# Induced attention and channel mix on one core: the running maximum meets across partitions on VectorE instead of TensorE

## The chip, the core and the metric

The kernel runs on one core of a Trainium2 chip. The metric is the device time of one execution in microseconds (us). Before the change three runs took 1166.9, 1169.22 and 1169.98 us, so the median is 1169.22. Engines go by the names of the profile: PE is TensorE (PEld its weight loads), DVE is VectorE, ACT is ScalarE, POOL is GpSimd, SP is SyncE, which issues the transfers.

## The reference

`x` holds 4 sequences of 12608 tokens with 128 channels, `inducing` 32 vectors. First the 32 vectors attend to all tokens of a sequence, which gives h (32 x 128); then each token attends to h. A channel mix follows on that result.

```python
def mab(q, kv):
    s = scale * (q @ kv.transpose(0, 2, 1))
    s = s - s.max(-1, keepdims=True)
    a = np.exp(s)
    a /= a.sum(-1, keepdims=True) + 1e-09
    return a @ kv
h = mab(I, x)                  # 32 queries over 12608 tokens
x = mab(x, h)                  # every token over 32 vectors
x_prev = x shifted by one token (zero in front)
xk = mu_k * x + (1.0 - mu_k) * x_prev
xr = mu_r * x + (1.0 - mu_r) * x_prev
k = np.maximum(xk @ w_k, 0.0)  # 1024 wide
v = k * k @ w_v
out = v / (1.0 + np.exp(-(xr @ w_r)))
```

The change concerns the maximum `s.max` of the first attention, the one over all tokens of a sequence, for each of the 32 vectors.

## The kernel before

A sequence is cut into 6 full blocks of 2048 tokens (block 0 to 5) and a remainder of 320. A block has four groups of 512 tokens, so a sequence has 25 groups. The channel mix handles a group in four units, each for 256 of the 1024 hidden channels; 4 sequences make 400 units, and the program is one long loop over units with the order of all engines written out by hand.

In unit n the loop emits, in this order: for a group that is done, the gate `L809` on VectorE (product of the finished bank of `ps_v` and the sigmoid); `up`, four TensorE products `L773`, `L775` into one of two pairs of banks of `ps_a`; the entries of a table `early` (filled by `soon`); `square`: VectorE takes the positive part (`L785`, ps_a to k_t), ScalarE squares twice (`L790` rounded, `L791` exact; in some units `L787` on VectorE in place of `L790`), GpSimd subtracts the two (`L793`, both inputs in SBUF); in one of four units `zgate`, the gate's product `L762`, `L763` into a bank of `ps_v`, of which there are two; `store` (`L820` and transfers); `down` of the unit four earlier, six products `L804` into the same `ps_v`; and then the entries of a table `events` (filled by `at`). An engine works through its instructions in this order, and SP its transfers.

The tables hold the attention work of later blocks. `stage_b` is the second attention of the block that the channel mix needs soon; its `low` (`L654`) splits off the low part of the weights from a bank `pb_b`, and its `spread` has SP send them to the tiles R that `up` reads. `stage_a` is the first attention of the next sequence, one block each 12 units, so it runs 18 times: blocks 0 to 5 of sequences 1 to 3 (sequence 0 has a head of its own, in which GpSimd has no subtractions). One such run is called a pass here. A pass starts at t; its scores are written in unit t + 9 to 128 partitions, 32 for each of the four groups of tokens, and `L364` takes the maximum over the free axis, which leaves one number per partition. The four numbers of one inducing vector lie in partitions m, m + 32, m + 64 and m + 96 and have to meet, since all four groups are to share one maximum. In block 5 the remainder's maximum `mxt` joins first (`L370`).

They meet in `common` and `running`. `common` has TensorE multiply the column of maxima, read as 128 equal columns, by the identity (`L371`; the profile counts two matmuls for it), so that each partition holds all 128 numbers in bank `pb_b`. `running` adds the constant `apart` (zero where the vector is the same, a huge negative number elsewhere, `L377`), and reduces by maximum (`L380`) together with the running maximum of earlier blocks, which lies in column 128 of the same tile; `L382` scales it to the bias `nb` of the exponentials in unit t + 15. `common` stands in `early` of unit t + 11, between `up` and `down`; in block 5 of unit t + 12; `running` in `events` of the same unit.

Of the kernel before, what the change touches and what calls it, by code (L numbers as in the profile page):

```python
# [8 lines left out]
F32 = mybir.dt.float32  # L9
# [4 lines left out]
ALU = mybir.AluOpType  # L14
AX = mybir.AxisListType
# [4 lines left out]
def kernel(  # L20
# [11 lines left out]
    nc = tc.nc  # L32
    B, N, C = x.shape
    M = inducing.shape[0]
    F = w_k.shape[1]
    P = 128
# [11 lines left out]
    scale = 1.0 / float(C) ** 0.5  # L48

    const = ctx.enter_context(tc.tile_pool(name="const", bufs=1))  # L50
# [4 lines left out]
    sm = ctx.enter_context(tc.tile_pool(name="sm", bufs=2))  # L55
# [7 lines left out]
    def pb_tile(bank=None):  # L63

        return pb.tile([P, G], F32, name="pb_" + (bank or next(banks)))


    ident = const.tile([P, P], F32, name="ident")
# [70 lines left out]
    omur = const.tile([P, 1], F32, name="omur")  # L139
    stack = const.tile([P, Q, M], F32, name="stack")  # L140
    stack_f = stack.rearrange("p i m -> p (i m)")
    apart = const.tile([P, P], F32, name="apart")

    def constants():
        for dst, src in ((omuk, muk), (omur, mur)):
            nc.vector.tensor_scalar(out=dst, in0=src, scalar1=-1.0, scalar2=1.0,
                                    op0=ALU.mult, op1=ALU.add)
        nc.vector.tensor_reduce(out=stack[:, 0, :], in_=ident.rearrange("p (i m) -> p m i", i=Q),
                                op=ALU.add, axis=AX.X)
        for i in range(1, Q):  # L150
            nc.vector.tensor_copy(out=stack[:, i, :], in_=stack[:, 0, :])
        nc.vector.tensor_scalar(out=apart, in0=stack_f, scalar1=-1.0, scalar2=3.0e38, op0=ALU.add, op1=ALU.mult)

    wvh = const.tile([P, FC, C], F32R, name="wvh")
    wvl = const.tile([P, FC, C], F32R, name="wvl")
# [158 lines left out]
    def stage_a(b, j, at, t):  # L314
# [2 lines left out]

        S = batches[b]
        L = {}
        tail = j == NBLK - 2
# [41 lines left out]
            L["mx"] = mx  # L365

        def common():
            ps = pb_tile("b")
            if tail:
                nc.vector.tensor_tensor(out=L["mx"], in0=L["mx"], in1=L["mxt"], op=ALU.max)  # L370
            nc.tensor.matmul(out=ps[:, :P], lhsT=L["mx"].broadcast_to([P, P]), rhs=ident,  # L371
                             start=True, stop=True)
            L["cp"] = ps

        def running():
            mk = S.mk if j > 0 else sm.tile([P, P + 1], F32, name="mkr", bufs=2)
            nc.vector.tensor_tensor(out=mk[:, :P], in0=L["cp"][:, :P], in1=apart, op=ALU.add)  # L377
            S.mk = sm.tile([P, P + 1], F32, name="mkr", bufs=2)
            L["mx"] = S.mk[:, P:P + 1]
            nc.vector.tensor_reduce(out=L["mx"], in_=mk[:, :P + (j > 0)], op=ALU.max, axis=AX.X)  # L380
            L["nb"] = sm.tile([P, 1], F32, name="nb")
            nc.vector.tensor_scalar(out=L["nb"], in0=L["mx"], scalar1=-scale, scalar2=None, op0=ALU.mult)  # L382

        def expo():
            e1t = st.tile([P, G], F32, name="e1t", bufs=1)
# [61 lines left out]
        if tail:  # L447
            at(t + 5, t_tr)
            soon(t + 11, t_scores)
        at(t + 9, scores)  # L450
        soon(t + 11 + tail, common)
        at(t + 11 + tail, running)
        at(t + 15, expo)
        at(t + 17, etrans)
# [440 lines left out]
    def head():  # L895
# [6 lines left out]
        for k in range(NBLK):  # L902
            ab[k].maxi()
            ab[k].expo()
            place(PARTS[k][0])
            if k > 0:
                ab[k - 1].hmm()
            if k == last:
                maxes()
            if k > 0:  # L910
                ab[k - 1].acc()
            if k == 0:
                constants()
            if k + 2 < NBLK:
                ab[k + 2].tr()
            place(PARTS[k][1])
            ab[k].etrans()
            ab[k].ecopy()
            ab[k].sums()
            if k < last:  # L920
                ab[k + 1].scores()
            place(PARTS[k][2])
# [13 lines left out]
    def at(n, f):  # L936
        events.setdefault(n, []).append(f)

    def soon(n, f):
        early.setdefault(n, []).append(f)  # L940
# [41 lines left out]
    for b in range(B):  # L982
        t = b * UB + (4 if b == 0 else 0)
        for j in range(NBLK - 1):
            s = t + SEG * j
            high_vector |= {s + 4, s + 8}
            if b + 1 < B:
                stage_a(b + 1, j, at, s)
            stage_b(b, j + 1, at, s + 1)
        if b + 1 < B:  # L990
            s = t + SEG * (NBLK - 1)
            combine(b + 1, at, s)
            stage_b(b + 1, 0, at, s + 13)
# [73 lines left out]
```

## Time and profile before

| | |
|---|---|
| median of 3 runs | 1169.22 us |
| profiled execution | 1165.47 us, its span 1163.7 us |
| mean granted TensorE clock | 0.996 |
| PE busy | 1114.2 us (96%) |
| ACT busy | 970.9 us (83%) |
| POOL busy | 947.7 us (81%) |
| DVE busy | 934.3 us (80%) |

The profile is of one execution. In its rows a group of instructions stands with line, engine, operation, tiles (written <- read), shape and count, then busy time and the mean of one in ns, then the idle time of the engine before them with what ended it. A row of the timeline begins with start and length in us. A row of a line's view gives shortest, median and longest duration in ns. The end of a matmul is modelled, so neighbours on PE overlap in the rows.

### The profile page before, as it was taken

The page shows a single profiled execution, that of the slowest core. Times are in us where ns is not written, and L with a number is a line of the kernel's source. Part 1 is how long each engine was busy: PE and PEld are TensorE (multiplying, and loading weights), DVE is VectorE, ACT ScalarE, POOL GpSimd, SP SyncE. Part 2 cuts the span into 40 slices and gives each one's busy share as a digit, 9 for nine tenths or more (in the row PEclk, how much of TensorE's full clock was granted, in tenths as well). Part 3 has the DMA queues.
Part 4 walks back from the last instruction along what each step waited for, and adds up shares of the span by engine and source line. Part 5 has one row for each costly group of instructions (what it writes and reads, how often), then busy time and mean ns, then how long its engine had stood idle before and what let it go on. Part 6 is the DMA issues. An engine that isn't in the chain of part 4 may idle for free.

```text
span 1163.7 us, 17576 instructions
## 1 busy us (share of the span) xinstructions
PE 1114.2 (96%) x5746; PEld 834.2 (72%) x5746; DVE 934.3 (80%) x1259; ACT 970.9 (83%) x1107; POOL 947.7 (81%) x413
## 2 busy tenths in 40 slices
PE   7779999999999999999999999999999999999997
PEld 5456777776677777777767777777768777777886
DVE  5778889887878888888787889897787888887665
ACT  5478888887888888788978988888789888889996
POOL 1158888888787888888879888888878899999997
PEclk9989999999999999999999999999999999999999
DMA  9112554544226455465043554645304314432231
GB/s 288 50 32 75 128 118 106 109 117 92 39 58 134 108 105 123 108 135 120 5 76 74 118 125 104 134 96 124 45 15 82 63 34 73 73 64 46 43 46 34
DMA packets 273515, 102.31 MB, mean 88 GB/s; under 512 B 232816, under 2 KB 248336, under 8 KB 271120
## 3 DMA queue, kind: packets, MB, share of 16 engines
q1 hardware_dynamic: 273088, 101.17, 40.5%
q8 instruction: 46, 0.75, 0.3%
q14 instruction: 45, 0.37, 0.1%
q10 hardware_dynamic: 336, 0.02, 0.0%
HBM read 28.07 MB, written 25.82 MB: 46 GB/s over the span
## 4 chain that ended last, share of the span: by engine, by line
PE 61%; DVE 15%; ACT 8%; SPq 6%; issue 5%; DMA 4%; DVEq 0%; ACTq 0%
PE ps_v L804 31%; PE ps_a L773 11%; PE ps_a L775 10%; DVE k_t L785 5%; SPq L336 2%; DMA out_dram<-ot 2%; ACT kh L790 2%; SPq L827 2%; PE pb_a L426 1%; PE pb_b L610 1%; PE ps_v L762 1%; PE ps_v L763 1%; SPq L664 1%; ACT k_t L791 1%; PE pb_a L361 1%
## 5 line engine op out<-in xcount | busy, mean ns | idle before, releaser
L793 POOL TENSOR_TENSOR kl<-k_t,kh 128x1024 fp32r<-128x1024 f32 (+2 forms) x400 | 939.0, 2375 | 169.0 <-ACT k_t L791 148.9
L785 DVE TENSOR_SCALAR k_t<-ps_a 128x1024 f32<-128x1024 f32 (+1 forms) x400 | 480.9, 1202 | 155.5 <-PE ps_a L775 144.1
L791 ACT ACTIVATE k_t<-k_t 128x1024 f32<-128x1024 f32 (+1 forms) x400 | 418.2, 1048 | 45.5 <-DVE kh L787 34.3
L790 ACT ACTIVATE kh<-k_t 128x1024 fp32r<-128x1024 f32 (+1 forms) x352 | 365.9, 1040 | 104.5 <-DVE k_t L785 57.8
L773 PE MATMUL ps_a<-R,W 128*128 128x512 f32 (+1 forms) x800 | 325.9, 408 | 4.7 <-DMA R<-al 3.4
L775 PE MATMUL ps_a<-R,W 128*128 128x512 f32 (+1 forms) x800 | 313.6, 392 | 0.0
L804 PE MATMUL ps_v<-kh,wvh 128*128 128x512 f32 (+1 forms) x800 | 251.9, 396 | 5.5 <-ACT rT L765 5.0
L804 PE MATMUL ps_v<-kl,wvh 128*128 128x512 f32 (+1 forms) x800 | 249.2, 393 | 0.0
L804 PE MATMUL ps_v<-kh,wvl 128*128 128x512 f32 (+1 forms) x800 | 249.0, 392 | 0.0
L773 PEld LDWEIGHTS ps_a<-R,W 128*128 128x128 f32 x800 | 151.2, 189 | 82.3 <-issue 22.4
L804 PEld LDWEIGHTS ps_v<-kh,wvh 128*128 128x128 f32 x800 | 147.9, 189 | 42.3 <-ACT rT L765 10.1
L804 PEld LDWEIGHTS ps_v<-kl,wvh 128*128 128x128 f32 x800 | 149.6, 188 | 35.5 <-POOL kl L793 0.3
L804 PEld LDWEIGHTS ps_v<-kh,wvl 128*128 128x128 f32 x800 | 149.8, 188 | 34.9
L775 PEld LDWEIGHTS ps_a<-R,W 128*128 128x128 f32 x800 | 151.1, 189 | 29.8
L820 DVE STREAM_TRANSPOSE ot<-oT 128x512 f32<-128x512 f32 x96 | 67.4, 702 | 12.2 <-DMA out_dram<-ot 11.3
L809 DVE TENSOR_TENSOR oT<-ps_v,rT 128x512 f32<-128x512 f32 (+1 forms) x100 | 66.7, 667 | 2.4 <-PE ps_v L804 0.2
L787 DVE SCALAR_TENSOR_TENSOR kh<-ps_a,k_t 128x1024 fp32r<-128x1024 f32 x48 | 58.8, 1225 | 5.4 <-PE ps_v L804 0.5
L765 ACT ACTIVATE rT<-ps_v 128x512 f32<-128x512 f32 (+1 forms) x99 | 57.2, 578 | 0.3
L333 DVE STREAM_TRANSPOSE xs<-xb 128x512 f32<-128x512 f32 x72 | 50.0, 695 | 0.3
L765 ACT ACT_TABLE_LOAD x31 | 39.8, 1283 | 0.6
L762 PE MATMUL ps_v<-R,W 128*128 128x512 f32 (+1 forms) x99 | 38.9, 393 | 0.0
L763 PE MATMUL ps_v<-R,W 128*128 128x512 f32 (+1 forms) x99 | 38.7, 391 | 0.0
(194 smaller groups left out, 643.6 us busy)
## 6 DMA issues: line engine op xcount, KB each, us to landing
out_dram<-ot SPq DMA_DIRECT2D x92, 256.0 KB, 4.4
xb<-in_x_dram SPq DMA_DIRECT2D x18, 1024.0 KB, 5.3
xt<-xs SPq DMA_DIRECT2D x288, 64.0 KB, 2.0
R<-ah SPq DMA_DIRECT2D x184, 64.0 KB, 2.0
R<-al SPq DMA_DIRECT2D x184, 64.0 KB, 2.0
kh<-in_x_dram SPq DMA_DIRECT2D x4, 512.0 KB, 8.2
kl<-in_x_dram SPq DMA_DIRECT2D x4, 512.0 KB, 6.4
xb<-in_x_dram SPq DMA_DIRECT2D x8, 256.0 KB, 5.4
```

What stands on the lines that cost most here:

```text
L762: nc.tensor.matmul(out=ps[:, :w], lhsT=S.W[0][:, F:WF], rhs=R[:, 1:w + 1], start=True, stop=False)
L765: nc.scalar.activation(out=self.rT, in_=ps[:, :w], func=AF.Sigmoid)
L773: nc.tensor.matmul(out=ps[:, c, :w], lhsT=S.W[0][:, cs], rhs=R[:, 1:w + 1], start=True, stop=False)
L775: nc.tensor.matmul(out=ps[:, c, :w], lhsT=S.W[1][:, cs], rhs=R[:, 0:w], start=False, stop=True)
L785: nc.vector.tensor_scalar(out=k, in0=self.ps[:, :, :w], scalar1=0.0, scalar2=None, op0=ALU.max)
L787: nc.vector.scalar_tensor_tensor(out=kh, in0=self.ps[:, :, :w], scalar=0.0, in1=k, op0=ALU.max, op1=ALU.mult)
L790: nc.scalar.activation(out=kh, in_=k, func=AF.Square)
L791: nc.scalar.activation(out=k, in_=k, func=AF.Square)
L793: return lambda eng, a, z: eng.tensor_tensor(out=kl[:, :, a:z], in0=k[:, :, a:z], in1=kh.bitcast(F32)[:, :, a:z], op=ALU.subtract)
L804: nc.tensor.matmul(out=self.v, lhsT=wt[:, fc, :], rhs=kk[:, c, :], start=(fc == 0 and n == 0), stop=(fc == FC - 1 and n == 2))
L809: nc.vector.tensor_tensor(out=self.oT, in0=self.v, in1=self.rT, op=ALU.mult)
L820: nc.vector.transpose(out=ot[:, o:o + w], in_=self.oT)
```

## The change

The product on TensorE, the constant `apart`, the addition and the reduction go. In their place the upper 64 partitions are compared with the lower 64 (`mh`), then, from block 1 on, the first 32 of the result with the running maximum, then its two halves of 32; the result stands in partitions 0 to 31 of a new [128,1] tile. `running` copies it to partitions 32 to 63, and these 64 to the upper 64, and scales as before. `common` moves from `early` of unit t + 11 to `events` of unit t + 10 (block 5: t + 12 to t + 11); `running` stays.

```diff
-    apart = const.tile([P, P], F32, name="apart")
...
-        nc.vector.tensor_scalar(out=apart, in0=stack_f, scalar1=-1.0, scalar2=3.0e38, op0=ALU.add, op1=ALU.mult)
...
         def common():
-            ps = pb_tile("b")
+
+            v, half = nc.vector, P // 2
             if tail:
-                nc.vector.tensor_tensor(out=L["mx"], in0=L["mx"], in1=L["mxt"], op=ALU.max)
-            nc.tensor.matmul(out=ps[:, :P], lhsT=L["mx"].broadcast_to([P, P]), rhs=ident,
-                             start=True, stop=True)
-            L["cp"] = ps
+                v.tensor_tensor(out=L["mx"], in0=L["mx"], in1=L["mxt"], op=ALU.max)
+            mh = sm.tile([half, 1], F32, name="mh", bufs=1)
+            v.tensor_tensor(out=mh, in0=L["mx"][:half], in1=L["mx"][half:], op=ALU.max)
+            L["mx"] = sm.tile([P, 1], F32, name="mkr", bufs=2)
+            if j > 0:
+                v.tensor_tensor(out=mh[:M], in0=mh[:M], in1=S.mrun[:M], op=ALU.max)
+            v.tensor_tensor(out=L["mx"][:M], in0=mh[:M], in1=mh[M:], op=ALU.max)
 
         def running():
-            mk = S.mk if j > 0 else sm.tile([P, P + 1], F32, name="mkr", bufs=2)
-            nc.vector.tensor_tensor(out=mk[:, :P], in0=L["cp"][:, :P], in1=apart, op=ALU.add)
-            S.mk = sm.tile([P, P + 1], F32, name="mkr", bufs=2)
-            L["mx"] = S.mk[:, P:P + 1]
-            nc.vector.tensor_reduce(out=L["mx"], in_=mk[:, :P + (j > 0)], op=ALU.max, axis=AX.X)
+            v, half = nc.vector, P // 2
+            v.tensor_copy(out=L["mx"][M:half], in_=L["mx"][:M])
+            v.tensor_copy(out=L["mx"][half:], in_=L["mx"][:half])
             L["nb"] = sm.tile([P, 1], F32, name="nb")
-            nc.vector.tensor_scalar(out=L["nb"], in0=L["mx"], scalar1=-scale, scalar2=None, op0=ALU.mult)
+            v.tensor_scalar(out=L["nb"], in0=L["mx"], scalar1=-scale, scalar2=None, op0=ALU.mult)
...
-        soon(t + 11 + tail, common)
+        at(t + 10 + tail, common)
         at(t + 11 + tail, running)
```

The line numbers of the changed kernel differ by up to three: L785 is L784 there, L654 is L653, L333 is L330, L809 is L808. Two places show the new order. The first is VectorE in a middle pass (blocks 1 to 4), from the L785 of unit t + 10 to the one of unit t + 12; `mx` is the block's maximum, `mkr` the running one. Before:

```order
L785 TENSOR_SCALAR k_t<-ps_a 128x1024
L654 TENSOR_TENSOR al<-pb_b,ah 128x512
L785 TENSOR_SCALAR k_t<-ps_a 128x1024
L377 TENSOR_TENSOR mkr<-pb_b,apart 128x128
L380 TENSOR_REDUCE mkr<-mkr 128x1
L382 TENSOR_SCALAR nb<-mkr 128x1
L333 STREAM_TRANSPOSE xs<-xb 128x512
L809 TENSOR_TENSOR oT<-ps_v,rT 128x512
L785 TENSOR_SCALAR k_t<-ps_a 128x1024
```

Now:

```order
L784 TENSOR_SCALAR k_t<-ps_a 128x1024
L370 TENSOR_TENSOR mh<-mx_2202 64x1
L373 TENSOR_TENSOR mh<-mh,mkr 32x1
L374 TENSOR_TENSOR mkr<-mh 32x1
L653 TENSOR_TENSOR al<-pb_b,ah 128x512
L784 TENSOR_SCALAR k_t<-ps_a 128x1024
L378 COPY mkr<-mkr 32x1
L379 COPY mkr<-mkr 64x1
L381 TENSOR_SCALAR nb<-mkr 128x1
L330 STREAM_TRANSPOSE xs<-xb 128x512
L808 TENSOR_TENSOR oT<-ps_v,rT 128x512
L784 TENSOR_SCALAR k_t<-ps_a 128x1024
```

Three maxima now stand ahead of the split L653 and of the next L784, and two copies stand where the addition and the reduction were; L373 is missing in a block 0. The second place is VectorE in a pass with the remainder (block 5), from the L785 of unit t + 11 on. Before:

```order
L785 TENSOR_SCALAR k_t<-ps_a 128x1024
L809 TENSOR_TENSOR oT<-ps_v,rT 128x512
L370 TENSOR_TENSOR mx_2927<-mx_2927,mx_2961 128x1
L785 TENSOR_SCALAR k_t<-ps_a 128x1024
L377 TENSOR_TENSOR mkr<-pb_b,apart 128x128
```

Now:

```order
L368 TENSOR_TENSOR mx_2933<-mx_2933,mx_2967 128x1
L370 TENSOR_TENSOR mh<-mx_2933 64x1
L373 TENSOR_TENSOR mh<-mh,mkr 32x1
L374 TENSOR_TENSOR mkr<-mh 32x1
L808 TENSOR_TENSOR oT<-ps_v,rT 128x512
L784 TENSOR_SCALAR k_t<-ps_a 128x1024
```

The maximum with the remainder moved from behind the gate to ahead of it, and three more follow it before the gate. On TensorE the rows L371 between `up` and `down` are gone, and nothing else moved.

## The prediction

> **What bounds the kernel now.** I read the page first, then the groups of TensorE from 65 us on, then the timeline of single passes, engine by engine. Times in rows are microseconds from the span's start: start, length, engine, line.
>
> ```profile
> PE 1114.2 (96%) x5746; PEld 834.2 (72%) x5746; DVE 934.3 (80%) x1259; ACT 970.9 (83%) x1107; POOL 947.7 (81%) x413
> L371 PE MATMUL pb_b<-ident,mx 128*128 128x128 f32 x36 | 7.4, 288 | 6.0 <-DVE mx L370 4.0 <-DVE al L654 1.9
> ```
>
> TensorE sets the time; the others have 17 to 20% to spare, so the question is what TensorE gains and whether VectorE (DVE) then makes it wait. The second row is what goes: 36 matmuls (18 products of two passes), before which TensorE stood still 6.0 us, 4.0 of them for the max L370 of the three passes with a remainder, 1.9 for L654, which still read bank b. What a product costs besides is seen in a middle pass, sequence 1, block 3:
>
> ```profile
> 206.89 0.39 PE L775 MATMUL ps_a<-R,W 128*128 128x512 f32 x1
> 207.11 0.38 PE L371 MATMUL pb_b<-ident,mx 128*128 128x128 f32 x2
> 207.25 0.71 PE L804 MATMUL ps_v<-kh,wvh 128*128 128x512 f32 x2
> 207.80 0.63 PE L804 MATMUL ps_v<-kh,wvl 128*128 128x512 f32 x2
> 209.44 0.40 PE L775 MATMUL ps_a<-R,W 128*128 128x512 f32 x1
> 209.67 0.62 PE L804 MATMUL ps_v<-kh,wvh 128*128 128x512 f32 x2
> 210.13 0.62 PE L804 MATMUL ps_v<-kh,wvl 128*128 128x512 f32 x2
> 212.00 0.39 PE L762 MATMUL ps_v<-R,W 128*128 128x512 f32 x1
> ```
>
> From the last L775 to the first wvl pair it is 207.80 - 206.89 = 0.91 us with the product and 210.13 - 209.44 = 0.69 without: 0.22 us each. L762, the next gate product, is the first TensorE instruction there that waits for a late VectorE, because it takes the ps_v bank that L809 reads.
>
> **What is taken away.** 18 x 0.22 = 4.0 us of slots and 6.0 us of waits, at most 10.0 us of TensorE. On VectorE an addition and a reduction go, 0.28 and 0.29 us in the rows below with a gap of 0.03. The constant apart, made once while VectorE waited for the first blocks, I cost at nothing either way: were its cover gone, it would be one 128x128 operation like L377, 0.28 us.
>
> **What is added, and what one costs.** Two [64,1] or [32,1] maxima of SBUF operands in a block 0, three in blocks 1 to 4, four (one old) in a block 5, then two copies. Nothing in the trace has their shapes; the nearest are these:
>
> ```profile
> L247 DVE TENSOR_TENSOR mx<-mx,mx x6: 158/159/160, 16.9 to 40.4; 128x1 f32<-128x1 f32 x6
> L370 DVE TENSOR_TENSOR mx<-mx,mx x3: 1239/1272/1927, 277.8 to 827.8; 128x1 f32<-128x1 f32 x3
> 277.84 1.93 DVE L370 TENSOR_TENSOR mx<-mx,mx 128x1 f32<-128x1 f32 x1
> 277.39 2.36 POOL L793 TENSOR_TENSOR kl<-k_t,kh 128x1024 fp32r<-128x1024 f32 x1 [1.88 <-ACT k_t L791]
> L519 DVE TENSOR_SCALAR h4k<-hT,omuk x4: 1301/2423/2427, 47.6 to 858.7; 128x128 f32<-128x128 f32 x4
> 80.62 2.40 POOL L793 TENSOR_TENSOR kl<-k_t,kh 128x1024 fp32r<-128x1024 f32 x1 [1.59 <-issue]
> 81.35 0.14 DVE L589 CAST R<-R 128x1 fp32r<-128x1 f32 x1
> ```
>
> The same one-element max takes 0.16 us in the head, where GpSimd (POOL) is idle, and 1.24 to 1.93 us later. The one at 277.84 ends at 279.77, 0.02 us after POOL's subtraction (277.39 + 2.36 = 279.75): it waits for that whole instruction. L519, SBUF to SBUF while POOL works without a pause, lasts 2.42 us, a whole POOL operation. So a max of SBUF operands costs 0.16 us when POOL is idle, the rest of POOL's operation when it isn't, and up to 2.4 us if POOL's next one is ready. I take 0.16 with a gap of 0.04, bounds 0.16 and 2.4. The Trainium skill, "SBUF — State Buffer", section "SBUF: two separate sides", says the same of a DVE operation with two SBUF inputs against GpSimd: an exclusive lock, held for a whole instruction; the rows agree.
>
> For a copy the nearest row is the cast of one element a partition: 0.14 us at 81.35, in the middle of a POOL operation. I take 0.14, upper bound the same wait. The same section of the skill counts an fp32 SBUF-to-SBUF copy among the two-port operations that take the lock; for one element the row speaks against it. By the rule the time would be that of the rival "copies wait" below.
>
> **A middle pass, worked through.** Sequence 1, block 3, and the last of its kind, sequence 3, block 2:
>
> ```profile
> 205.07 1.23 DVE L785 TENSOR_SCALAR k_t<-ps_a 128x1024 f32<-128x1024 f32 x1 [0.39 <-PE ps_a L775]
> 206.21 0.68 DVE L654 TENSOR_TENSOR al<-pb_b,ah 128x512 fp32r<-128x512 f32 x1
> 207.38 1.23 DVE L785 TENSOR_SCALAR k_t<-ps_a 128x1024 f32<-128x1024 f32 x1 [0.49 <-PE ps_a L775]
> 208.53 0.28 DVE L377 TENSOR_TENSOR mkr<-pb_b,apart 128x128 f32<-128x128 f32 x1
> 208.84 0.29 DVE L380 TENSOR_REDUCE mkr<-mkr 128x1 f32<-128x129 f32 x1
> 209.16 0.15 DVE L382 TENSOR_SCALAR nb<-mkr 128x1 f32<-128x1 f32 x1
> 209.27 0.71 DVE L333 STREAM_TRANSPOSE xs<-xb 128x512 f32<-128x512 f32 x1
> 209.91 0.65 DVE L809 TENSOR_TENSOR oT<-ps_v,rT 128x512 f32<-128x512 f32 x1
> 198.57 9.51 POOL L793 TENSOR_TENSOR kl<-k_t,kh 128x1024 fp32r<-128x1024 f32 x4 [1.55 <-ACT k_t L791]
> 208.67 4.79 POOL L793 TENSOR_TENSOR kl<-k_t,kh 128x1024 fp32r<-128x1024 f32 x2 [0.59 <-ACT k_t L791]
> 720.25 1.23 DVE L785 TENSOR_SCALAR k_t<-ps_a 128x1024 f32<-128x1024 f32 x1 [0.40 <-PE ps_a L775]
> 713.71 9.49 POOL L793 TENSOR_TENSOR kl<-k_t,kh 128x1024 fp32r<-128x1024 f32 x4 [1.55 <-ACT k_t L791]
> ```
>
> The maxima stand behind L785, which ends at 206.30. POOL is busy until 198.57 + 9.51 = 208.08 and starts again at 208.67, when ScalarE has made the squares of that L785. So the first max waits 1.80 us, to 208.10; the second ends at 208.30, the third at 208.50, in POOL's pause. Queued behind them is L654, then the next L785, the copies, L333, L809. L654 ends at 209.10, L785 runs 209.02 to 210.25 (1.64 late), copies and nb take 0.14, 0.14 and 0.15 us against 0.78 for the three old ones, and L809 ends at 211.94 instead of 210.56. L762 stood at 212.00 and would now come at 211.78: a stall of 0.16 us, most of the 0.22 gained. The next bank of ps_a and the kl have more room. In sequence 3, block 2, POOL ends 1.72 us after L785 (723.20 against 721.48). I count six such passes at 0.15, 0.9 us together; the six other middle ones, where POOL ends sooner, keep all.
>
> **The passes that cost more.**
>
> ```profile
> 103.60 0.68 DVE L654 TENSOR_TENSOR al<-pb_b,ah 128x512 fp32r<-128x512 f32 x1
> 107.63 0.46 PE L773 MATMUL ps_a<-R,W 128*128 128x512 f32 x1 [1.31 <-DMA R<-al]
> 97.92 14.22 POOL L793 TENSOR_TENSOR kl<-k_t,kh 128x1024 fp32r<-128x1024 f32 x6 [1.57 <-ACT k_t L791]
> 374.99 1.23 DVE L785 TENSOR_SCALAR k_t<-ps_a 128x1024 f32<-128x1024 f32 x1 [0.52 <-PE ps_a L775]
> 369.81 18.99 POOL L793 TENSOR_TENSOR kl<-k_t,kh 128x1024 fp32r<-128x1024 f32 x8 [1.57 <-ACT k_t L791]
> 381.94 0.40 PE L762 MATMUL ps_v<-R,W 128*128 128x512 f32 x1
> 653.08 1.23 DVE L785 TENSOR_SCALAR k_t<-ps_a 128x1024 f32<-128x1024 f32 x1 [0.39 <-PE ps_a L775]
> 648.51 18.98 POOL L793 TENSOR_TENSOR kl<-k_t,kh 128x1024 fp32r<-128x1024 f32 x8 [1.58 <-ACT k_t L791]
> 276.09 1.22 DVE L785 TENSOR_SCALAR k_t<-ps_a 128x1024 f32<-128x1024 f32 x1
> 282.56 0.40 PE L762 MATMUL ps_v<-R,W 128*128 128x512 f32 x1
> 548.79 2.38 POOL L793 TENSOR_TENSOR kl<-k_t,kh 128x1024 fp32r<-128x1024 f32 x1 [1.20 <-ACT k_t L791]
> ```
>
> In the blocks 0 POOL has no pause: its operations follow each other every 2.37 us. Sequence 1: boundaries at 105.03 and 107.40, so the two maxima end at 105.05 and 107.42, and L654 ends at 108.06 instead of 104.28. Here L654 has no room: its SyncE transfers fill the R for which TensorE already waited until 107.63. They come 3.8 us later, and so does everything; the 0.22 gained lies inside that wait. Sequence 2: L785 ends at 376.22, the boundaries are 376.93 and 379.31, the maxima end at 379.33. By the middle pass L809 ends 3.44 us behind the last max, at 382.77; L762 would be at 381.72: 1.05 us lost. Sequence 3: 658.02 is 3.71 us behind its L785, 0.60 more than in sequence 2, so 1.65.
>
> The passes with a remainder (block 5): in sequence 1, L785 ends at 277.31; POOL starts at 277.39 and goes straight on (the old L370 sat there to 279.77), so the maxima run to 279.77, 282.1 and 282.3, L809 to 283.0; L762, 2.0 us earlier for the wait and slot removed, would be at 280.56: 2.4 lost. In sequences 2 and 3 I let all four pass: POOL ends at 551.17, then three more to 551.79, the last begun at 551.63, and POOL's next starts 2.37 behind L785's end of 549.38, at 551.75. This is the tightest place, 0.12 us.
>
> **Sum.** Gained 17 x 0.22 + 6.0 = 9.7; lost 0.9 + 3.8 + 1.05 + 1.65 + 2.4 = 9.8: plus 0.1 us. Against the profiled execution's own 1165.47 that is 1165.6; its span is 1163.7. Against the median of the three runs, 1169.22 (3.7 above), it is 1169.3.
>
> **Rivals.**
>
> *Alternation (faster).* After one wait VectorE gets its next max in before POOL's next operation. Then sequence 1 loses 1.6 in block 0 (L654 ends 105.9) and 0.3 in block 5, sequences 2 and 3 nothing, the middle passes 0.9: 9.7 - 2.8 = 6.9 gained, 1162.3. For it: POOL needs 0.13 us after its squares in most pauses; against it: L519 with the two whole waits in a row. 0.25.
>
> *The last max slips behind POOL's next start (slower).* Place: blocks 5 of sequences 2 and 3, where 0.12 us decide; price: the max ends at POOL's end, about 554.2, L809 at 554.8, and L762, brought forward to 552.6, loses 2.2: 4.4 for two, 1173.7. If a small max across partitions costs twice L247's 0.16, the third one of the middle passes, with 0.33 us to spare, goes too: six passes, L809 at 2.4 + 2.37 + 3.44 = 8.2 behind L785 instead of 5.6, 2.6 each, 15.6 more: 1189.3. For it: no row shows operands in different partitions; against it: the middle passes look alike to 0.1 us and leave room. 0.27.
>
> *Copies wait (slower).* In a middle pass the first copy at 210.2 would wait for POOL's end at 211.07, 0.8 us more to L809 in up to nine passes where L762 then has no room: about 7 us, 1176.4. Against it stands the cast at 81.35. 0.08.
>
> No change as summed: 0.40.
>
> **Numbers.** About 0.3%, 3.5 us, is what these runs can tell from no change. Faster 0.25, same 0.40, slower 0.35. The range takes the alternation, just, at the bottom and the doubled cost nearly at the top: 1160.5 to 1188. The forecast's own range is 1165.7 to 1172.7.
>
> **What will show it.** Right: no L371; L370 at about 1.8 us, L373 and L374 at 0.16 in middle passes; the two maxima of sequence 1, block 0, near 1.4 and 2.3 us, and the up product behind at about 111.4; the copies at 0.14; POOL's lengths unchanged. Wrong: a third max of about 2 us in middle passes, copies over 1 us, or a first max of 0.16 us in the middle of a POOL operation, which would leave most of the 10 us as gain.

## The result and the profile after

The changed kernel takes 1198.08 us (median of four runs, 1194.75 to 1199.21) against 1168.70 for the kernel before on the same chip (four runs): a ratio of 1.0249, 95% interval 1.0226 to 1.0273. It is slower by 29 us. The prediction said 1169.3 us, "the same", in a range up to 1188; the time lies outside it. Of the runs behind all the numbers below, one, of the kernel with the maxima one unit later, took 2163 us against 1236 to 1237 of its others; it is not explained, and the ratio leaves it out.

The page of the changed kernel, profiled in an execution of 1199.21 us (a span of 1197.4): the engines, then one group of instructions.

```profile
PE 1127.2 (94%) x5710; PEld 840.2 (70%) x5710; DVE 961.0 (80%) x1309; ACT 968.7 (81%) x1107; POOL 946.8 (79%) x413
L819 DVE STREAM_TRANSPOSE ot<-oT 128x512 f32<-128x512 f32 x96 | 67.3, 701 | 34.2 <-DMA out_dram<-ot 34.2
```

The 36 matmuls are gone (5710 for 5746), but TensorE was busy 13 us longer, at a mean granted clock of 0.980 for 0.996. And a line that neither the change nor the prediction touches now waits for much longer: L819 writes a finished group into the output tile `ot`. On the page of before the same line read:

```profile
L820 DVE STREAM_TRANSPOSE ot<-oT 128x512 f32<-128x512 f32 x96 | 67.4, 702 | 12.2 <-DMA out_dram<-ot 11.3
```

So VectorE waited 11.3 us for output stores before, and 34.2 us after. These numbers are the start of the explanation. First, though, what came as forecast. The three maxima of the changed kernel, line by line (shortest, median and longest in ns), and VectorE in sequence 1, block 3:

```profile
L370 DVE TENSOR_TENSOR mh<-mx x18: 153/1471/2246, 108.8 to 863.6; 64x1 f32<-64x1 f32 x18
L373 DVE TENSOR_TENSOR mh<-mh,mkr x15: 147/147/149, 151.7 to 863.7; 32x1 f32<-32x1 f32 x15
L374 DVE TENSOR_TENSOR mkr<-mh x18: 147/147/2322, 110.2 to 863.9; 32x1 f32<-32x1 f32 x18
```

```profile
216.57 1.22 DVE L784 TENSOR_SCALAR k_t<-ps_a 128x1024 f32<-128x1024 f32 x1 [0.41 <-PE ps_a L774]
217.83 1.76 DVE L370 TENSOR_TENSOR mh<-mx 64x1 f32<-64x1 f32 x1
219.62 0.15 DVE L373 TENSOR_TENSOR mh<-mh,mkr 32x1 f32<-32x1 f32 x1
219.80 0.15 DVE L374 TENSOR_TENSOR mkr<-mh 32x1 f32<-32x1 f32 x1
220.11 0.69 DVE L653 TENSOR_TENSOR al<-pb_b,ah 128x512 fp32r<-128x512 f32 x1 [0.15 <-ACT k_t L790]
221.96 0.14 DVE L378 COPY mkr<-mkr 32x1 f32<-32x1 f32 x1
```

A first max of 1.76 us, two of 0.15, a copy of 0.14, and L653 ending 3.01 us behind the L784 ahead of it (220.80 against 217.79), where the prediction had 2.80. In block 0 of sequence 1 two maxima of 1.32 and 2.29 us stand ahead of L653, and TensorE (second fence, one view) waits for R:

```profile
108.84 1.32 DVE L370 TENSOR_TENSOR mh<-mx 64x1 f32<-64x1 f32 x1
110.20 2.29 DVE L374 TENSOR_TENSOR mkr<-mh 32x1 f32<-32x1 f32 x1
```

```profile
116.60 0.76 PE L772 MATMUL ps_a<-R,W 128*128 128x512 f32 x1 [5.39 <-DMA R<-al]
117.16 0.63 PE L774 MATMUL ps_a<-R,W 128*128 128x512 f32 x1
117.59 0.63 PE L772 MATMUL ps_a<-R,W 128*128 128x512 f32 x1
118.01 0.63 PE L774 MATMUL ps_a<-R,W 128*128 128x512 f32 x1
```

The wait of 5.39 us is 4.1 more than the 1.31 of before (the prediction had R 3.8 us later and the 0.22 of the slot inside the wait, 4.0 together). But the products behind it start 0.43 us apart, and before they started 0.24 apart: the clock is at half. That is the second thing the prediction doesn't contain.

**Where the 33.7 us between the two spans arose.** The first `up` product of unit n starts later than before by 3.5 us in unit 0 (the head, which also differs by some us from run to run), 5.1 in unit 10, 11.2 in unit 20, 11.5 in unit 50, 14.1 in unit 60, 18.0 in unit 80, 24.4 in unit 150, 28.2 in unit 220, 33.6 in unit 250, 33.7 in the last. The largest steps are at the wait for R of unit 16 (6.0 us with the half clock behind it) and near units 57, 73, 141, 157 and 241, where VectorE waits for an output store; at unit 257 that wait grew too, but the lag is the same on both sides of it. Unit 57 in the two kernels, first before (the transfers of the store on SP's queue, then VectorE, then TensorE), then after, where L330 and the first `xt` transfers of the pass stand ahead of these:

```profile
218.27 5.55 SPq L827 DMA_DIRECT2D out_dram<-ot  x4
227.24 0.71 DVE L820 STREAM_TRANSPOSE ot<-oT 128x512 f32<-128x512 f32 x1 [1.89 <-DMA out_dram<-ot]
227.88 0.67 DVE L405 STREAM_TRANSPOSE e<-e1t 128x512 f32<-128x512 f32 x1
228.60 0.65 PE L426 MATMUL pb_a<-xb,e 128*32 128x128 f32 x16 [1.23 <-DVE e L405]
```

```profile
222.43 0.71 DVE L330 STREAM_TRANSPOSE xs<-xb 128x512 f32<-128x512 f32 x1
223.17 2.41 SPq L333 DMA_DIRECT2D xt<-xs  x4
228.89 2.43 SPq L333 DMA_DIRECT2D xt<-xs  x4
231.42 6.68 SPq L826 DMA_DIRECT2D out_dram<-ot  x4
241.38 0.71 DVE L819 STREAM_TRANSPOSE ot<-oT 128x512 f32<-128x512 f32 x1 [4.17 <-DMA out_dram<-ot]
242.01 0.67 DVE L404 STREAM_TRANSPOSE e<-e1t 128x512 f32<-128x512 f32 x1
242.74 0.64 PE L425 MATMUL pb_a<-xb,e 128*32 128x128 f32 x16 [3.54 <-DVE e L404]
```

Read it as a chain. `ot` has one buffer of four groups. SP stores it with four transfers and VectorE may write the next group only when these have landed. Counted from the end of the pass's L785 or L784 (206.30 before, 217.79 after), the store is issued at 11.97 before and at 13.63 after. SP works through its queue in order, and from the `xt` transfers at 223.17 on it comes to the store without a pause of more than 0.2 us. Those transfers wait for the late L330, which ends at 223.14; the spreads of the late L653 are through by then. The issue of the store then takes 1.13 us longer, and so L819 waits 4.17 us for 1.89. Behind L819 on VectorE stands the transpose `e` of the first attention, for which TensorE's L425 waits: 3.54 us for 1.23. At the other five units (73, 141, 157, 241 and 257) VectorE's wait grew from 0.8 to 2.7 us to 4.3 to 5.7 us.

**The store itself takes longer, everywhere.** The 5.55 us above is the longest issue of all 23 stores of four 256 KB transfers in the trace of before; the others take 4.05 to 5.30. In the changed kernel all 23 take 5.74 to 6.81. That holds in the last sequence too, where no pass runs and nothing is late: first a store there in the kernel before, then in the changed one, then the page's rows of these transfers (KB, and median us from issue to landing) of the two.

```profile
999.88 4.05 SPq L827 DMA_DIRECT2D out_dram<-ot  x4
1033.71 6.01 SPq L826 DMA_DIRECT2D out_dram<-ot  x4
out_dram<-ot SPq DMA_DIRECT2D x92, 256.0 KB, 4.4
out_dram<-ot SPq DMA_DIRECT2D x92, 256.0 KB, 5.2
```

From the first issue to the last landing a store takes 7.8 us in the median before and 9.6 after. At the six units above that is 9.4 us together, half of the 18.3 us by which VectorE's waits there grew; the rest is the later issue. So there are two ways to the longer wait, and the longer store is one that a late max does not explain.

### The profile page after: what moved, and what is told of

Read it like the earlier page. It is cut to its first block, busy times and chain, and to the rows that moved or that the text cites. A ratio compares the mean times of both kernels' runs of the same rounds, so it can differ in the third digit from the quotient of the medians.

```text
span 1197.4 us, 17554 instructions
## 1 busy us (share of the span) xinstructions
PE 1127.2 (94%) x5710; PEld 840.2 (70%) x5710; DVE 961.0 (80%) x1309; ACT 968.7 (81%) x1107; POOL 946.8 (79%) x413
## 4 chain that ended last, share of the span: by engine, by line
PE 62%; DVE 16%; ACT 7%; issue 5%; DMA 5%; SPq 4%; DVEq 0%; ACTq 0%
PE ps_v L803 30%; PE ps_a L772 12%; PE ps_a L774 10%; DVE k_t L784 6%; DMA out_dram<-ot 3%; SPq L826 2%; ACT kh L789 2%; PE pb_a L425 2%; PE pb_b L609 2%; PE ps_v L761 2%; PE pb_a L358 1%; PE ps_v L762 1%; ACT k_t L790 1%; DVE oT L808 1%; ACT L764 1%
## 5 line engine op out<-in xcount | busy, mean ns | idle before, releaser
L784 DVE TENSOR_SCALAR k_t<-ps_a 128x1024 f32<-128x1024 f32 (+1 forms) x400 | 479.9, 1200 | 130.3 <-PE ps_a L774 120.0
L772 PE MATMUL ps_a<-R,W 128*128 128x512 f32 (+1 forms) x800 | 330.3, 413 | 13.4 <-DMA R<-al 7.9
L774 PE MATMUL ps_a<-R,W 128*128 128x512 f32 (+1 forms) x800 | 317.0, 397 | 0.0
L772 PEld LDWEIGHTS ps_a<-R,W 128*128 128x128 f32 x800 | 153.0, 191 | 93.8 <-issue 23.0
L803 PEld LDWEIGHTS ps_v<-kh,wvh 128*128 128x128 f32 x800 | 150.8, 191 | 44.1 <-ACT rT L764 9.6
L774 PEld LDWEIGHTS ps_a<-R,W 128*128 128x128 f32 x800 | 153.2, 192 | 30.0
L819 DVE STREAM_TRANSPOSE ot<-oT 128x512 f32<-128x512 f32 x96 | 67.3, 701 | 34.2 <-DMA out_dram<-ot 34.2
L808 DVE TENSOR_TENSOR oT<-ps_v,rT 128x512 f32<-128x512 f32 (+1 forms) x100 | 66.6, 666 | 2.2
L330 DVE STREAM_TRANSPOSE xs<-xb 128x512 f32<-128x512 f32 x72 | 50.0, 694 | 0.4 <-issue 0.3
L762 PE MATMUL ps_v<-R,W 128*128 128x512 f32 (+1 forms) x99 | 38.7, 391 | 0.0
```

Of the source, the lines that this page charges most:

```text
L772: nc.tensor.matmul(out=ps[:, c, :w], lhsT=S.W[0][:, cs], rhs=R[:, 1:w + 1], start=True, stop=False)
L774: nc.tensor.matmul(out=ps[:, c, :w], lhsT=S.W[1][:, cs], rhs=R[:, 0:w], start=False, stop=True)
L784: nc.vector.tensor_scalar(out=k, in0=self.ps[:, :, :w], scalar1=0.0, scalar2=None, op0=ALU.max)
L803: nc.tensor.matmul(out=self.v, lhsT=wt[:, fc, :], rhs=kk[:, c, :], start=(fc == 0 and n == 0), stop=(fc == FC - 1 and n == 2))
L808: nc.vector.tensor_tensor(out=self.oT, in0=self.v, in1=self.rT, op=ALU.mult)
L819: nc.vector.transpose(out=ot[:, o:o + w], in_=self.oT)
```

## The experiments

**The lock, taken away and doubled.** The first kernel makes the four maxima of two SBUF tensors into operations of one tensor and one scalar per partition; place and number stay. The second leaves them as they are and puts them one unit later, where the prediction's view of GpSimd's instructions has no pause for the later ones.

```diff
-                v.tensor_tensor(out=L["mx"], in0=L["mx"], in1=L["mxt"], op=ALU.max)
+                v.tensor_scalar(out=L["mx"], in0=L["mx"], scalar1=L["mxt"], scalar2=None, op0=ALU.max)
...
-            v.tensor_tensor(out=mh, in0=L["mx"][:half], in1=L["mx"][half:], op=ALU.max)
+            v.tensor_scalar(out=mh, in0=L["mx"][:half], scalar1=L["mx"][half:], scalar2=None, op0=ALU.max)
...
-                v.tensor_tensor(out=mh[:M], in0=mh[:M], in1=S.mrun[:M], op=ALU.max)
-            v.tensor_tensor(out=L["mx"][:M], in0=mh[:M], in1=mh[M:], op=ALU.max)
+                v.tensor_scalar(out=mh[:M], in0=mh[:M], scalar1=S.mrun[:M], scalar2=None, op0=ALU.max)
+            v.tensor_scalar(out=L["mx"][:M], in0=mh[:M], scalar1=mh[M:], scalar2=None, op0=ALU.max)
```

> The small maxima take their second operand as a one-element scalar per partition (the form of L415, 0.25 us in the middle of a GpSimd operation) and not as a second tensor. Same work, same order, same count. If the wait for GpSimd is the cause: each small max lasts 0.16 to 0.26 us in every pass, L653 is 0.5 to 0.8 us late instead of 1.6 to 8, the wait of the store's transpose L819 falls from 34 us to 12 to 18, and the time is 1158 to 1166, faster than before. If it is the count of the small operations or their place ahead of L653: 1190 to 1200, as with two tensors.

```diff
-        at(t + 10 + tail, common)
+        at(t + 11 + tail, common)
```

> The maxima are moved behind the L784 of unit t + 11, directly ahead of the copies; L653 no longer stands behind them. If only the late L653 (its transfers to R and the stores behind them on SyncE) costs the time: back to 1160 to 1172. If the wait for GpSimd costs wherever it stands: GpSimd starts its next subtraction 0.06 us after that L784 and goes on without a pause, so two of the three maxima wait for a whole operation, about 5 us a pass, the gate L808 comes some 3 us too late for TensorE in most passes, and the time is 1205 to 1240, slower than the change.

Measured: 1182.43 us with the scalar form, ratio 1.0112 [1.0095, 1.0128]; 1237.17 us one unit later, ratio 1.0578 [1.0560, 1.0596]. The lines of the two kernels, and of the first one the row of the output tile:

```profile
L370 DVE TENSOR_SCALAR mh<-mx x18: 207/208/210, 108.1 to 847.1; 64x1 f32<-64x1 f32 x18
L819 DVE STREAM_TRANSPOSE ot<-oT 128x512 f32<-128x512 f32 x96 | 67.3, 701 | 30.7 <-DMA out_dram<-ot 30.7
```

```profile
L373 DVE TENSOR_TENSOR mh<-mh,mkr x15: 147/2259/2368, 147.5 to 897.7; 32x1 f32<-32x1 f32 x15
L374 DVE TENSOR_TENSOR mkr<-mh x18: 147/2280/2320, 108.5 to 900.1; 32x1 f32<-32x1 f32 x18
```

The mechanism of the prediction holds: with one tensor operand a max takes 0.21 us in all 18 passes, with two it waits until GpSimd's instruction ends, and one unit later two of them do in most passes (2.26 and 2.28 us). But without a single such wait the kernel is still 13 us slower than before. Lifting the wait brought back 16 of 29 us; 30.7 us of waits for stores stayed, where 12 to 18 were expected, and the time lies between the two that were expected. One unit later came out as expected.

**The meeting removed altogether.** This kernel leaves the product and what replaced it out, so that each partition keeps its own maximum (only the maximum with the remainder stays, at the change's place ahead of the gate, and waits 1.9 us for GpSimd in two of its three passes): a partition then has exponentials scaled by its own bound, and the four groups of tokens are no longer under one. It asks what the removed product and its waits are worth at most.

```diff
         def common():
...
-            mh = sm.tile([half, 1], F32, name="mh", bufs=1)
-            v.tensor_tensor(out=mh, in0=L["mx"][:half], in1=L["mx"][half:], op=ALU.max)
...
-            v.tensor_copy(out=L["mx"][M:half], in_=L["mx"][:M])
-            v.tensor_copy(out=L["mx"][half:], in_=L["mx"][:half])
```

> Leaves out the meeting of the maxima: neither product nor small maxima nor copies; each partition keeps its own maximum of its own block. This is the time without any of it. From the profile before: 6.0 us of waits and 4.0 us of slots less, 1157 to 1161. If the removal of the product gives nothing, 1168; if the loss of the change comes from something else than the small operations, up to 1190.

Measured: 1171.01 us, ratio 1.0019 [1.0007, 1.0030]. The expectation was 10 us too low. With next to nothing added, the 9.7 us which the prediction counts as gained are not gained. The page and the timeline of this kernel show one place where time was lost:

```profile
L811 DVE STREAM_TRANSPOSE ot<-oT 128x512 f32<-128x512 f32 x96 | 67.4, 702 | 27.6 <-DMA out_dram<-ot 27.6
231.16 0.85 PE L417 MATMUL pb_a<-xb,e 128*32 128x128 f32 x16 [1.85 <-DVE e L396]
```

VectorE waits 27.6 us for output stores instead of 11.3, and TensorE's wait behind one of them, the 1.23 us of before, is 1.85. Nothing is late in SP's queue here, but the stores are as long as in the changed kernel (issue 5.65 to 7.76 us): at the six units they take 9.4 us longer together than before, and VectorE's waits there grew by 10.2. A later experiment takes the store out.

**One small max, added to the kernel before.** Nothing else is changed; the result is not used. It stands where the change put its first max, ahead of the split.

```diff
+        def extra():
+            mh = sm.tile([P // 2, 1], F32, name="mh", bufs=1)
+            nc.vector.tensor_tensor(out=mh, in0=L["mx"][:P // 2], in1=L["mx"][P // 2:], op=ALU.max)
+
+        at(t + 10 + tail, extra)
         soon(t + 11 + tail, common)
```

> The kernel before, with nothing removed and one operation more in each pass: the max of the two halves of the partitions (two SBUF tensors, [64,1]), ahead of L654, its result not used. If the wait for GpSimd is the cause: it lasts 1 to 2 us in most passes, L654 and with it SyncE's queue come as late, and the time is 1180 to 1195. If it is only an operation of 0.16 us, VectorE has room for 18 of them: 1167 to 1171.

Measured: 1201.83 us, ratio 1.0299 [1.0266, 1.0333]. The direction is as expected, the size is not.

```profile
L453 DVE TENSOR_TENSOR mh<-mx 64x1 f32<-64x1 f32 x18 | 21.3, 1186 | 0.6
L825 DVE STREAM_TRANSPOSE ot<-oT 128x512 f32<-128x512 f32 x96 | 67.4, 702 | 27.3 <-DMA out_dram<-ot 27.2
```

18 operations of 1.19 us in the mean, 21 us of an engine that is idle a fifth of the time, cost 33 us. Here the product waits too: its bank is the one the split still reads, and it stood 0.9 to 2.8 us in 17 of 18 passes, 25.7 us together for 6.0 in the kernel before. So most of these 33 us is a cost that the changed kernel, which has no product, doesn't have. The stores are long here as well (5.80 to 7.48 us of issue), though only one small operation was added to the kernel before.

**The output tile in two halves.** This takes the store out of the argument: two tiles of two groups in place of one of four, with the same memory, and each stored when its two groups are there. One kernel is the one before with this edit, one the changed kernel with it.

```diff
...
-            elif g % Q == 0:
+            elif g % 2 == 0:
                 self.S.ot = out_tile()
...
-            o = (g % Q) * G
+            o = (g % 2) * G
...
-            span = 1 if self.b == B - 1 and g // Q == NBLK - 2 else Q
+            span = 1 if self.b == B - 1 and g // Q == NBLK - 2 else 2
...
-        return mp.tile([P, Q * G], F32, name="ot", bufs=1)
+        return mp.tile([P, 2 * G], F32, name="ot", bufs=2)
```

> The kernel before, with the output tile of four groups cut into two tiles of two groups (same memory, two buffers in place of one, stores of two groups each). Nothing else. If TensorE's product was never worth anything because the store behind SyncE's queue sets the time in the middle blocks: the transpose L820 no longer waits for its store (11 us before) and the time falls a little, 1160 to 1167. If those waits were hidden: 1167 to 1171.

> The changed kernel with the same two output tiles. If the late L653 costs its time by way of the stores (SyncE issues them later, the transpose L819 waits 34 us, TensorE behind it, then the halved clock): 1172 to 1185, with the wait of 5.4 us for R in sequence 1, block 0, left. If the waits for GpSimd cost directly, by late k_t and gates: 1192 to 1200.

Measured: the kernel before with this edit 1161.83 us, ratio 0.9941 [0.9921, 0.9961]; the changed one 1175.97, ratio 1.0064 [1.0043, 1.0086]. Both as expected. The row of the output tile in the first, and TensorE in block 0 of sequence 1 in the second:

```profile
L820 DVE STREAM_TRANSPOSE ot<-oT 128x512 f32<-128x512 f32 x96 | 67.3, 701 | 0.0
```

```profile
113.25 0.76 PE L772 MATMUL ps_a<-R,W 128*128 128x512 f32 x1 [5.29 <-DMA R<-al]
113.81 0.63 PE L774 MATMUL ps_a<-R,W 128*128 128x512 f32 x1
```

No wait for a store is left in either. The edit is worth 6.9 us to the kernel before and 22.1 to the changed one, so the change costs 29 us with the single tile and 14 without: half of the loss runs through the wait for the store. Part of what remains is seen in the second fence: the wait for R, with the clock at half behind it.

**The place.** Scalar maxima as above, but entered behind the split in the same unit, so that the split is on time. First with the single output tile, then with the split one.

```diff
-        at(t + 10 + tail, common)
+        L["meet"] = lambda: at(t + 10 + tail, common)
+        meets.append(L["meet"])
...
             stage_b(b, j + 1, at, s + 1)
+            run(meets)
+            del meets[:]
```

> The kernel with scalar operands (1182.4), with the maxima of blocks 0 to 4 placed directly behind the split L654 of the same unit in place of ahead of it; everything else in its order. If the 0.7 us by which L654 comes late is what those six small operations cost: 1168 to 1174, as with no meeting of the maxima at all (1171.0). If their own time on VectorE costs it: 1180 to 1184.

> The previous one with the two output tiles. If both reasons hold and add up, the product's 6 us of waits and 4 us of slots come out at last: 1155 to 1163, faster than the kernel before. If SyncE's queue is the bound also without the wait for the store: 1164 to 1171.

Measured: 1179.40 us, ratio 1.0095 [1.0071, 1.0120], a miss; and with the split tile 1157.56 us, ratio 0.9901 [0.9878, 0.9924], as expected and faster than both kernels. In the miss the split is on time, yet stores were waited for 32.5 us. Its store ahead of unit 57 on SP's queue:

```profile
223.49 6.22 SPq L827 DMA_DIRECT2D out_dram<-ot  x4
```

Relative to its L785 the store is issued at 12.07 (before 11.97), so it is not late; its issue lasts 6.22 us for 5.55. In the kernel without any meeting the issue came at 11.29 and lasted 6.5. A late queue is thus not needed for the wait: the split tile takes back 21.8 us of this kernel, whose queue is on time, and 22.1 of the changed one. What the kernels with the single tile share is the long store: 5.65 us of issue or more in each store of the six kernels that differ from the one before, 5.55 or less there. With the split tile it is the same: from issue to landing a transfer takes 2.7 us in the median in the kernel before and 3.3 in the others. In these traces it goes with the kernel and not with the chip, since the kernel before and the changed one with the split tile ran on the same chip. Every kernel but those two has other small tiles than the kernel before, so its tiles may lie at other addresses; whether that is the reason was not tested.

**What each part costs with the store out of the way.** Three more kernels with the split tile: without any meeting, with the scalar maxima at the change's place, and with the change's own maxima of two tensors behind the split. Each is a kernel above with the edit of the output tile; the last keeps the changed kernel's `common` and takes the edit of the place.

```diff
-        return mp.tile([P, Q * G], F32, name="ot", bufs=1)
+        return mp.tile([P, 2 * G], F32, name="ot", bufs=2)
```

> Leaves out the meeting of the maxima (each partition keeps its own) and has the two output tiles. With the waits for the store gone, taking the product away should show its worth: by the profile 6 to 9 us below the kernel before with two output tiles (1161.8), 1152 to 1157. If the product's removal is worth nothing in itself: 1160 to 1163.

> Scalar operands and two output tiles, the maxima ahead of L653 as in the change. If the place ahead of L653 costs only by way of SyncE's stores: 1157 to 1160, as behind L654 (1157.6). If the late L653 costs by itself too: 1161 to 1166.

> Two second tensors as in the change, but the maxima behind the split L654, and two output tiles. What is left then is the wait for GpSimd by itself, on the way to the next L784 and to the gate. If it is hidden there: 1157 to 1161, as with scalar operands. If it costs by itself: 1164 to 1172.

| with the split output tile | us | ratio to before, 95% |
|---|---|---|
| before | 1161.83 | 0.9941 [0.9921, 0.9961] |
| no meeting at all | 1158.75 | 0.9902 [0.9887, 0.9917] |
| scalar maxima, ahead of the split | 1158.16 | 0.9894 [0.9881, 0.9908] |
| scalar maxima, behind it | 1157.56 | 0.9901 [0.9878, 0.9924] |
| maxima of two tensors, behind it | 1166.38 | 0.9979 [0.9968, 0.9990] |
| maxima of two tensors, ahead (the change) | 1175.97 | 1.0064 [1.0043, 1.0086] |

The product and its waits are worth 3 to 5 us (3.1 by the times, 4.6 by the ratios, each to the kernel before on its own chip), not 10; the expectation for the kernel without meeting had two ranges, and the time lies between them. Maxima that don't wait for GpSimd are free in either place. The wait for GpSimd costs 8 to 9 us by itself, and another 9 to 10 when the split stands behind it. In the trace without any meeting TensorE gains 1.6 us on the kernel before (both with the split tile) in each of the three passes with a remainder, 4.8 together, and loses 2.0 at one place. That is block 0 of sequence 1, on TensorE, first in the kernel before with the split tile, then without any meeting:

```profile
109.51 0.47 PE L773 MATMUL ps_a<-R,W 128*128 128x512 f32 x1 [1.35 <-DMA R<-al]
109.81 0.39 PE L775 MATMUL ps_a<-R,W 128*128 128x512 f32 x1
```

```profile
109.92 0.47 PE L764 MATMUL ps_a<-R,W 128*128 128x512 f32 x1 [2.27 <-DMA R<-al]
110.23 0.40 PE L766 MATMUL ps_a<-R,W 128*128 128x512 f32 x1
110.47 0.44 PE L764 MATMUL ps_a<-R,W 128*128 128x512 f32 x1
110.70 0.63 PE L766 MATMUL ps_a<-R,W 128*128 128x512 f32 x1
```

R comes when its transfers land. TensorE, earlier by the slot removed, waits 2.27 us instead of 1.35, and that was long enough to bring the clock down for the products behind.

**The clock.** The changed kernel with the split tile, and 26 transposes of the identity into an idle bank while TensorE waits for R in block 0 of sequence 1; nobody reads them.

```diff
+        if b == 1 and j == 0:
+            def fill():
+                ps = pb_tile("b")
+                for _ in range(26):
+                    nc.tensor.transpose(out=ps[:, :P], in_=ident, identity=ident)
+            at(t + 11, fill)
```

> The changed kernel with two output tiles (1176.0) and 26 idle transposes on TensorE while it waits for R in sequence 1, block 0; nothing else. If a long idle stretch of TensorE is what halves its clock afterwards: the window of half clock behind that place is gone, the products there stand 0.23 us apart and not 0.43, and the time is 1 to 3 us less, 1173 to 1175. If the half clock has another cause: it stays, 1176 to 1179.

Measured: 1175.01 us, ratio 1.0040 [1.0028, 1.0053], not to be told apart from the 1175.97 without the fill. The timeline of TensorE shows what was asked:

```profile
110.15 4.72 PE L456 MATMUL pb_b<-ident 128*128 128x128 f32 x26 [1.95 <-DVE al L659]
114.64 0.47 PE L778 MATMUL ps_a<-R,W 128*128 128x512 f32 x1
114.95 0.39 PE L780 MATMUL ps_a<-R,W 128*128 128x512 f32 x1
115.18 0.40 PE L778 MATMUL ps_a<-R,W 128*128 128x512 f32 x1
```

The same products run 0.23 us apart, where they ran 0.43 apart without the fill: the half clock there comes from TensorE's idleness, not from its load. The fill ended too late and held the `up` product behind it up by 1.1 us (it starts 1.39 us later than without the fill, in traces 0.25 us apart until then), and unit 20 began only 0.9 us sooner, so as a remedy it gives nothing that can be measured.

## Why the prediction was wrong

**What held.** The lock and its size (1.76 us in a middle pass for 1.80), the price of the others (0.15 for 0.16), copies that don't wait (0.14), the two maxima of block 0 (1.32 and 2.29 for about 1.4 and 2.3), a wait for R 4.1 us longer for 4.0. In block 5 of sequences 2 and 3 the old maximum waited 1.9 us and the three others took 0.15 each, as forecast; in sequence 1 one of the four waited (2.25 us) where two were forecast. The rival "copies wait" is out, and so is a doubled price for operands in different partitions. The Trainium skill, "SBUF — State Buffer", section "SBUF: two separate sides", was right on the two-input operations: the traces here agree (0.15 us or the rest of GpSimd's instruction, up to 2.3 us). What that section counts among the operations that can take the lock, a copy and an operation of one tensor and a scalar, waited in none of the 18 passes with one number a partition (0.14 and 0.21 us).

**The step that failed first: the path behind the max.** The prediction wrote "Queued behind them is L654, then the next L785, the copies, L333, L809", and followed only L809, to the gate L762. Of L654 and L333 it followed the transfers only in block 0 of sequence 1, where TensorE waits for R. It has no term for the output store, which stands behind these transfers on SP in six of the passes, and whose single buffer VectorE needs back before it can do the transpose that TensorE waits for: it is put at nothing without a reason. The trace of before already showed this wait: 11.3 us on L820, six times, and a TensorE gap of 1.23 us at 228.60. The split output tile shows what it was worth: it takes back 22.1 us of the changed kernel and 6.9 of the one before, so 15 of the 29 us come through the store. That the wait grew has two reasons in the traces, the later issue (1.66 us at unit 57) and the longer store (7.8 to 9.6 us, in every kernel but the one before). How the 15 us divide between them is not shown; the kernel with the queue on time lost as much to the store, so the late queue alone does not account for them.

**The second: the gain of 17 x 0.22 + 6.0 = 9.7.** It takes the removed slots and waits at full value. Removing them alone gave nothing with the single output tile (1.0019), and 3 to 5 us with the split one. Part of the time saved was seen to end at the next thing that comes at its own time: R in block 0 of sequence 1 (1.35 to 2.27 us), and the store. The prediction saw this for one pass ("The 0.22 gained lies inside that wait") and didn't ask it for the others.

**The third: the loss of 9.8 at full clock.** The waits for GpSimd cost 8 to 9 us behind the split and 18 ahead of it, without the store. A part of the surplus is the clock: in the changed kernel five stretches of 3.4 or 6.8 us behind the head, 30.7 us together, ran at half. TensorE was busy for 24.7 us of them; at twice the length of each product that makes about 12 us, an estimate from the windows of the trace and an upper bound, as not all of it was on the chain that ended last. The gates' waits of 0.3 to 0.6 us in seven middle passes, for six of 0.15 predicted, are a smaller part.

Of the rivals, "the last max slips" had the right sign and the wrong place: no third max slipped (L374's median is 147 ns). Alternation came in one of three blocks 0: in sequence 2 the first max waited (1.60 us) and the second took 0.15, but in sequences 1 and 3 both waited, the second for 2.29 and 2.32.

**Still open.** Why the store takes longer in every kernel but the one before, also where nothing delays it, and what that alone costs. How the 10 us between the maxima of two tensors behind the split and ahead of it divide: between the traces of these two kernels with the split tile, 3.7 us arise at the wait for R of unit 16 and the half clock behind it, and the rest in small steps of 0.4 to 1.5 us along the run.

## What to carry to other kernels

When an operation is put ahead of others on an in-order engine, follow everything it delays to its last consumer, through the queue of transfers to the buffer that these give back: here half of the loss went through an output tile that no one had touched. Compare also how long the untouched transfers themselves take in both traces; here each store had become 1.8 us longer, which no single place of the timeline shows. A wait that stands in the trace of before on a single buffer is a place where the next delay lands and where the next saving is lost; take that buffer out of the way first (two halves of the same memory gave 0.6% to the kernel before), and then ask what the change is worth. A max of one number a partition beside a busy GpSimd belongs into the form with one tensor and a scalar per partition: 0.21 us each time. In that form and with the split tile the change is 1.1% faster than before, 0.6 of it from the tile.

## What the runs showed of the hardware

**The clock goes by fixed periods.** All the stretches of half clock in one trace start on one grid of 3.41 us, and each lasts one or two of its periods (the one at the end of a run apart). In the changed kernel, windows cut along this grid (start and end, length, busy time and count of each engine, granted clock, DMA share, GB/s):

```profile
237.55:240.96 3.41, 1.64 (x8) 1.00 (x6) 0.00 (x0) 3.36 (x4) 3.19 (x2) 1.00 0.72 108
240.96:244.37 3.41, 1.63 (x21) 1.26 (x22) 2.99 (x5) 1.29 (x3) 1.38 (x1) 1.00 0.41 96
244.37:247.78 3.41, 3.41 (x29) 2.45 (x28) 3.31 (x7) 3.10 (x4) 1.61 (x1) 1.00 0.36 80
483.30:486.71 3.41, 1.38 (x6) 0.76 (x5) 0.00 (x0) 3.35 (x4) 3.18 (x2) 1.00 0.75 116
486.71:490.13 3.42, 1.55 (x17) 1.10 (x18) 2.91 (x5) 0.93 (x2) 1.09 (x1) 0.50 0.41 97
```

The wait of 3.54 us for the store of unit 57 falls into two periods, which leaves TensorE idle for 1.77 and 1.78 us in them, and the clock stays full. That of 3.89 us for the store of unit 141 leaves it idle for 2.03 us in one period, and the next runs at half. Over the 14 traces, without the first 72 and the last 15 us of each, there are some 4380 periods at full clock. TensorE was idle for 1.88 us or more in 39 of them, and each was followed by half clock. Five had 1.83 to 1.87 us, with two followed by half clock. None below was (in the last microseconds, left out here, one of 1.72 us was). A period at half clock was followed by another one where TensorE was idle for 0.71 us or more in it (9 times), and by full clock where it was idle for 0.23 us or less. So in these traces about 1.85 us of idleness within one period of 3.41 decides, and whether a gap of 2 to 3.7 us costs anything besides itself depends on where the grid happens to lie. This is a count made afterwards, apart from the one run with the fill, whose 1.95 us of idleness led to one period of half clock, as counted. The Trainium skill, "TensorE: Matmul & The Clock Gate", section "Part 1: The HAM clock gate (the "warmup" mystery)", gives a free-running window of 3413 ns, with which these traces agree, and half clock after at least one idle window; by these traces a little over half a window is enough.

**For one number a partition, the form decides on the wait for GpSimd.** A max of the same 64 or 32 numbers in the same place takes 0.15 us or up to 2.3 as an operation of two tensors, and 0.20 to 0.21 us always as one of a tensor and a scalar per partition, while GpSimd works. The form alone does not free a wider operation: L519 of the kernel before, one 128x128 tensor and a scalar per partition, lasts up to 2.43 us.
